# A two-layer linear-attention and gated-MLP kernel on one core: operations ordered by longest chain, and normalized rows transposed by DMA behind the first normalizations

## Chip, core and metric

The kernel runs on one core of a Trainium2 chip. The metric is device time of the whole program in microseconds (us). The time before is 454.07 us, the median of three runs (452.1, 454.07, 454.61). The engines are called as the profile calls them: PE (TensorE matmul), PEld (its weight load), DVE (VectorE), ACT (ScalarE), POOL (GpSimd), SP (SyncE, which here only issues DMAs).

## The reference

`x` is 2048 rows of 512 bf16 numbers. Two blocks alternate, A, B, A, B, with the same weights in both layers. `A_w_phi` holds one 16x16 matrix for each of 32 heads.

```python
def _A_ref(x, wqkv, w_phi, wo):                       # H = 32 heads of 16
    q, k, v = ((x @ wqkv) ... split into heads)
    pq = einsum("bhsd,hdf->bhsf", q, w_phi);  pk = einsum("bhsd,hdf->bhsf", k, w_phi)
    phi_q = concatenate([softmax(pq), softmax(-pq)]);  phi_k = concatenate([softmax(pk), softmax(-pk)])
    kv  = einsum("bhsf,bhsd->bhfd", phi_k, v);         z = sum of phi_k over s
    num = einsum("bhqf,bhfd->bhqd", phi_q, kv)
    den = einsum("bhqf,bhf->bhq", phi_q, z) + 1e-6
    return (num / den) ... heads joined ... @ wo

def _B_ref(x, W_gate, W_up, W_down):                  # F = 1376
    return (relu(x @ W_gate) * (x @ W_up)) @ W_down

x = x + _A_ref(layernorm(x), ...);  x = x + _B_ref(layernorm(x), ...)
x = x + _A_ref(layernorm(x), ...);  x = x + _B_ref(layernorm(x), ...)
```

`kv` and `z` sum over all 2048 rows, so no row can pass the second half of A before every row has passed the first half.

## The kernel before

**Tiling.** The rows are 16 tiles of 128, and 4 stages (`st`) of 4 tiles. All weights and `x` (`x_sb`) stay in SBUF. One row of work for a stage is this:

- `layernorm(st)` (lines 400 to 441). On DVE, per tile: statistics (line 404, 405), then for the four tiles together twelve tiny operations that make 1/sqrt(variance) by bit trick and two Newton steps (lines 415 to 423), then one `ytile <- x_sb` per tile (line 429, "apply"). PE transposes each `ytile` in four 128x128 blocks into one PSUM bank (line 318), and DVE (odd tiles, line 437) or ACT (even tiles, line 440) copies the bank into `yT`, which has rows of x along the free axis. `ytile` has 4 buffers, `yT` has 6 (each for a whole stage).
- `keys(st)`: per tile 4 + 4 matmuls of 128x512 (`Wkp`, `wv`), two exponentials on ACT (line 464), their sum and its reciprocal on DVE (466, 468), a copy of v on ACT (472), v over the sums on POOL (475); then 32 small matmuls `vhat,expk` that give this stage's share of `kv` and `z`, added into `kvsum` on DVE (488, 491).
- `sums()`: DVE turns `kvsum` into two matrices, `ZDw` and `kvbd` (500, 503). It needs all four stages.
- `queries(st)`: 16 matmuls with `Wqp` and eight exponentials on ACT (513). `Wqp` and `Wkp` are products of the weights with `w_phi`, made once at the start (`fold`).
- `attend(st)`: 32 tiny matmuls `ZDw,expq`; a chain on DVE (`Zs`, `zm`, `zden`, reciprocal `zr`, `atok`, lines 530 to 537); 4 PE transposes of `atok` and a copy `aT` (542); 8 matmuls `aT,EC`, each followed by a DVE multiply into `expq` (547, "em"); 8 matmuls `expq,kvbd`, copied to `oT` by ACT (552); 16 matmuls `wo_sb,oT`, each four of them added into `x_sb` on DVE (561, "residual").
- `glu(st)`: 88 matmuls with `Wg` and `Wu`, 11 relus on ACT (576), 11 multiplies on DVE (578), 44 matmuls `Wd,hT`, four residuals on DVE (561). All 88 need the four tiles of `yT`.

**Order.** The kernel does not write the instruction streams by hand. `op` and `dma` record operations with what they read and write and with an estimated occupancy and latency in ns; a `Program` derives dependences, lays all operations out in time (`schedule`) and makes from that the in-order stream and the semaphore waits of each engine (`plan`, `emit`). `schedule` takes, at each step, the operation that can begin first by its own estimates; among equals, the one recorded first (`prio` is the index). It also gives out the eight PSUM banks at that time, so an operation can wait for a bank that another stage's operation still reads. What is laid out is fixed: on the chip each engine runs its stream in order and waits at each semaphore.

The order in which operations are recorded (lines 602 to 617): layer 1's `layernorm` and `keys` of stages 0 to 3; then in each layer `sums`, queries and attend of stage 0 with the normalization behind it, and in turn queries and attend of stage st+1 (with its normalization), `glu(st)`, and the next layer's `layernorm` and `keys` of stage st (or, in layer 2, the four output DMAs of stage st, on SP). So there are 16 normalizations of a stage: 4 ahead of layer 1's keys, 4 ahead of layer 1's glu, 4 ahead of layer 2's keys, 4 ahead of layer 2's glu. SP has nothing to do between the loads at the start and the 16 output DMAs.

Of the kernel before, what the change touches and what calls it, by code (L numbers as in the profile page):

```python
# [42 lines left out]
class Op:  # L43
    __slots__ = ("idx", "eng", "fn", "reads", "writes", "occ", "lat", "name", "is_dma", "nbytes",
                 "deps", "odeps", "users", "missing", "ready", "start", "finish", "cnt", "stream", "prio")

    def __init__(self, idx, eng, fn, reads, writes, occ, lat, name, is_dma=False, nbytes=0):
        self.idx, self.eng, self.fn = idx, eng, fn
        self.reads, self.writes = list(reads), list(writes)
        self.occ, self.lat, self.name = float(occ), float(lat), name  # L50
        self.is_dma, self.nbytes = is_dma, nbytes
        self.deps, self.odeps, self.users = set(), set(), []
        self.missing, self.ready = 0, 0.0
        self.start = self.finish = self.cnt = self.stream = None
        self.prio = idx


class Program:
    SYNC = 120.0
    SAME = 60.0  # L60
# [12 lines left out]

    def dma(self, eng, fn, reads=(), writes=(), nbytes=0, name=""):
        o = Op(len(self.ops), eng, fn, reads, writes, self.DMA_ISSUE[eng], 0, name, True, nbytes)
        self.ops.append(o)
        return o

# [37 lines left out]

    def schedule(self):
        self.derive()
        free = {e: 0.0 for e in ENGINES}
# [3 lines left out]
        left = len(self.ops)  # L123
        for o in self.ops:
            if not o.missing:
                ready[o.eng].append(o)
# [4 lines left out]
        while left:  # L131
            best = None
            for e in ENGINES:
                for o in ready[e]:
                    s = max(free[e], o.ready)
                    if best is not None and s > best[0] and s > free[e]:
                        continue
                    b = new_bank(o)
                    if b is not None:
                        if not banks:  # L140
                            continue
                        s = max(s, min(banks)[0])
                    key = (s, o.prio)
                    if best is None or key < best[:2]:
                        best = (s, o.prio, o)
            assert best is not None, "no operation can go on"
            s, _, o = best
            ready[o.eng].remove(o)
            b = new_bank(o)
            if b is not None:  # L150
                entry = min(banks)
                banks.remove(entry)
                b.bank = entry[1]
                old = entry[2]
                if old is not None:
                    for x in old.ops:
                        if x.eng != "pe":
                            o.deps.add(x.idx)
            o.start = s
            if o.is_dma:  # L160
                free[o.eng] = s + o.occ
                begin = max(s + 0.35 * self.DMA_LAT, qfree)
                qfree = begin + o.nbytes / self.DMA_BW
                o.finish = qfree + 0.65 * self.DMA_LAT
            else:
                free[o.eng] = s + o.occ
                o.finish = s + o.lat
            for r in set(o.reads) | set(o.writes):
                if isinstance(r, Bank):
                    r.left -= 1  # L170
                    if not r.left:
                        t = max(x.finish + (0.0 if x.eng == "pe" else self.SYNC) for x in r.ops)
                        banks.append((t, r.bank, r))
            for u in o.users:
                if o.idx in u.deps:
                    t = o.finish + (self.SAME if u.eng == o.eng and not o.is_dma else self.SYNC)
                    u.ready = max(u.ready, t)
                u.missing -= 1
                if not u.missing:
                    ready[u.eng].append(u)  # L180
            left -= 1
# [57 lines left out]
def build_kernel(nc, A_x, A_wqkv, A_w_phi, A_wo, W_gate, W_up, W_down, out):  # L239
# [8 lines left out]
    with ExitStack() as ctx:  # L248
# [58 lines left out]
        op, dma = prog.op, prog.dma  # L307
# [4 lines left out]
        def mm(ps, view, lhsT, rhs, start, stop, reads, n, name):  # L312
            lat = 0.4167 * n + 167
            op("pe", lambda e: e.matmul(view(ps), lhsT, rhs, start=start, stop=stop),  # L314
               reads=reads, writes=[ps], occ=max(25.0, 0.4167 * n + 2.6), lat=lat, name=name)

        def tr(ps, view, src, reads, name):
            op("pe", lambda e: e.transpose(view(ps), src, ident[:]),  # L318
               reads=list(reads) + [R("ident")], writes=[ps], occ=56, lat=220, name=name)
# [4 lines left out]
        def b16half(ps):  # L324
            return ps.b16()[:, 0:512]

# [8 lines left out]
        def load_x(t0, t1):  # L335
# [27 lines left out]
           reads=[R("mask8a")], writes=[R("mask8")], occ=150, name="mask8")  # L363
        op("pool", lambda e: e.affine_select(EC[:].rearrange("p g (h j) -> p g h j", j=16), ones[:].rearrange("p (g h j) -> p g h j", g=8, j=16),
                                             [[-8, 8], [-1, 8], [0, 16]], ALU.is_equal, 0.0, base=0, channel_multiplier=1),
# [35 lines left out]
        def layernorm(st):  # L401

            for t in range(4 * st, 4 * st + 4):
                op("dve", (lambda t: lambda e: e.bn_stats(stats[:, t, :], x_sb[:, t, :]))(t), reads=[R("x", t)], writes=[R("st", t)], occ=580, lat=680, name=f"bn{t}")  # L404
                op("dve", (lambda t: lambda e: e.bn_aggr(mv[:, t, :], stats[:, t, :]))(t), reads=[R("st", t)], writes=[R("mv", t)], occ=70, lat=172, name=f"ba{t}")  # L405
            ts = range(4 * st, 4 * st + 4)
            var = mv[:, 4 * st:4 * st + 4, 1:2]
            y = rstd[:, 4 * st:4 * st + 4, :]
            v, hx, t1 = rsv[:, st], rsh[:, st], rst[:, st]
            Rmv, Ry, Rv, Rh, Rt = [R("mv", t) for t in ts], [R("rs", t) for t in ts], [R("rv", st)], [R("rh", st)], [R("rt", st)]  # L410

            def small(fn, reads, writes):
                op("dve", fn, reads=reads, writes=writes, occ=65, lat=160, name="rstd")

            small(lambda e: e.tensor_scalar(v, var, float(EPS_LN), None, op0=ALU.add), Rmv, Rv)
            small(lambda e: e.tensor_scalar(hx, var, 0.5, 0.5 * float(EPS_LN), op0=ALU.mult, op1=ALU.add), Rmv, Rh)
            small(lambda e: e.tensor_single_scalar(t1.bitcast(I32), v.bitcast(I32), 1, ALU.logical_shift_right), Rv, Rt)
            small(lambda e: e.tensor_scalar(y.bitcast(I32), t1.bitcast(I32), -1, 0x5F3759DF, op0=ALU.mult, op1=ALU.add), Rt, Ry)
            for _ in range(2):
                small(lambda e: e.tensor_tensor(t1, y, y, ALU.mult), Ry, Rt)  # L420
                small(lambda e: e.tensor_tensor(t1, t1, hx, ALU.mult), Rt + Rh, Rt)
                small(lambda e: e.tensor_scalar(t1, t1, -1.0, 1.5, op0=ALU.mult, op1=ALU.add), Rt, Rt)
                small(lambda e: e.tensor_tensor(y, y, t1, ALU.mult), Ry + Rt, Ry)
            b = cnt["yT"] % NYT
            cnt["yT"] += 1
            for t in ts:
                yb = cnt["y"] % NY
                cnt["y"] += 1
                op("dve", (lambda t, yb: lambda e: e.tensor_scalar(ytile[:, yb, :], x_sb[:, t, :], mv[:, t, 0:1], rstd[:, t, :], op0=ALU.subtract, op1=ALU.mult))(t, yb),  # L429
                   reads=[R("x", t), R("mv", t), R("rs", t)], writes=[R("y", yb)], occ=320, lat=405, name=f"apply{t}")  # L430
                ps = bank(f"ytr{t}")
# [4 lines left out]
                if tt % 2:  # L436
                    op("dve", (lambda ps, dst: lambda e: e.tensor_copy(dst, b16half(ps).rearrange("p (c n) -> p c n", c=NC)))(ps, dst),
                       reads=[ps], writes=[R("yT", b, tt)], occ=328, lat=415, name=f"ycp{t}")
                else:
                    op("act", (lambda ps, dst: lambda e: e.activation(dst, b16half(ps).rearrange("p (c n) -> p c n", c=NC), ACT.Copy))(ps, dst),  # L440
                       reads=[ps], writes=[R("yT", b, tt)], occ=480, lat=600, name=f"ycp{t}")
# [5 lines left out]
        def keys(st, b):  # L447
# [30 lines left out]
            for g0, g1 in ((0, 3), (3, 6), (6, 8)):  # L478
# [8 lines left out]
                if st == 0:  # L487
                    op("dve", (lambda ps, dst, n: lambda e: e.tensor_copy(dst, ps.f32()[:, 0:n]))(ps, dst, n),  # L488
                       reads=[ps], writes=[R("kvs", g0)], occ=490, lat=580, name="kvs")
# [26 lines left out]
        def attend(st):  # L516
# [13 lines left out]
            op("dve", lambda e: e.tensor_copy(Zs[:, g], zdv(zd)[:, :, 0]), reads=[zd], writes=[R("Zs", g)], occ=330, lat=420, name="Zs")  # L530
# [11 lines left out]
            op("dve", lambda e: e.tensor_copy(aT[:, g, :], b16half(pa)), reads=[pa], writes=[R("aT", g)], occ=328, lat=415, name="aT")  # L542
            for c in range(NC):
# [8 lines left out]
                op("act", (lambda c, pn: lambda e: e.activation(oT[:, g, c, :], full(pn), ACT.Copy))(c, pn), reads=[pn], writes=[R("oT", g, c)], occ=480, lat=610, name=f"oT{st}")  # L552
# [49 lines left out]
        for st in range(NS):  # L602
            into_a(st)
# [71 lines left out]
```

## Time and profile before

| | |
|---|---|
| runs | 452.1, 454.07, 454.61 us; median 454.07 |
| profiled execution | 453.24 us; its span in the profile is 451.5 us, so 1.74 us lie around the span |
| PE (matmul records) | 419.7 us, 93% of the span |
| DVE | 331.3 us, 73% |
| ACT | 182.0 us, 40% |
| POOL | 72.9 us, 16% |
| chain that ended last, by engine | PE 77%, DVE 19%, DMA 1%, ACT 1% |
| DMA | 10.95 MB, nearly all in the first 20 us |

A "busy" PE is not PE at its peak, since matmuls are pipelined and the record of one overlaps the next: a 128x512 matmul has a record of 379 ns, and they follow each other faster than that. PE's idle time is therefore read from the weight-load records (PEld), whose starts give the pace. Idle time in front of an instruction is given with what ended it: "[4.51 <-DVE aT L542]" is 4.51 us of idleness that ended when DVE's copy of line 542 was done.

### The profile page before, as it was taken

What the parts mean: (1) busy time and instruction counts of PE and PEld (TensorE: products, weight loads), DVE (VectorE), ACT (ScalarE), POOL (GpSimd) and SP (SyncE); (2) the same over time, 40 slices, a digit from 0 to 9 for tenths busy, and PEclk for the clock granted to TensorE, in tenths of its full rate; (3) what the DMA queues carried; (4) which work ended last, traced back from release to release, by engine and by line L of the source; (5) the groups of instructions that cost most, each with busy time, mean ns of one, the idle gap of its engine ahead of it and who ended that gap; (6) DMA issues with size and microseconds to landing.
All of it is one profiled execution on the core that took longest, in us unless ns stands there. A gap on an engine that the chain in (4) does not pass through costs nothing.

```text
span 451.5 us, 6587 instructions
## 1 busy us (share of the span) xinstructions
PE 419.7 (93%) x2512; PEld 211.2 (47%) x2560; DVE 331.3 (73%) x819; ACT 182.0 (40%) x329; POOL 72.9 (16%) x75
## 2 busy tenths in 40 slices
PE   3969899789999999999999999887999999999997
PEld 2545556334544544444445444632454454444443
DVE  5999977999669956997578476799963863883342
ACT  4768687223406440453145249622340340341230
POOL 3335780000000700070007005100000000000000
PEclk9999999979999999999999999988999999999999
DMA  8930000000000000000000000000001001000001
GB/s 260 384 107 1 0 1 2 1 0 1 0 1 2 1 1 0 2 0 1 0 1 1 1 0 1 1 1 1 0 2 46 1 0 37 12 1 23 23 1 46
DMA packets 9567, 10.95 MB, mean 24 GB/s; under 512 B 992, under 2 KB 8512, under 8 KB 9536
## 3 DMA queue, kind: packets, MB, share of 16 engines
q1 hardware_dynamic: 7952, 9.47, 6.1%
q10 hardware_dynamic: 1584, 1.07, 0.8%
q8 instruction: 20, 0.33, 0.3%
q14 instruction: 11, 0.09, 0.1%
HBM read 8.44 MB, written 2.10 MB: 23 GB/s over the span
## 4 chain that ended last, share of the span: by engine, by line
PE 77%; DVE 19%; DMA 1%; issue 1%; ACT 1%; POOL 0%; SPq 0%
PE pb L314 74%; DVE expq L547 4%; PE pb L318 3%; DVE stats L404 3%; DVE x_sb L561 2%; DVE Zk L466 1%; DMA x_sb<-in_A_x_dram 1%; DVE kvsum L491 1%; DVE ytile L429 1%; DVE zr L535 1%; DVE hT L578 1%; DVE kvsum L488 1%; DVE kvbd L503 0%; DVE mv L405 0%; DVE Zs L530 0%
## 5 line engine op out<-in xcount | busy, mean ns | idle before, releaser
L576 ACT ACTIVATE gate_sb<-pb 128x512 bf16<-128x512 f32 (+1 forms) x88 | 52.5, 596 | 138.3 <-PE pb L314 136.0
L475 POOL TENSOR_TENSOR vhat<-vsb,rZk 128x544 bf16<-128x544 bf16 x64 | 68.5, 1102 | 210.6 <-DVE rZk L468 195.4
L578 DVE TENSOR_TENSOR hT<-gate_sb,pb 128x512 bf16<-128x512 bf16 (+1 forms) x88 | 59.8, 680 | 44.0 <-PE pb L314 43.8
L314 PE MATMUL pb<-yT,Wg 128*128 128x512 bf16 (+1 forms) x340 | 91.1, 379 | 0.4
L314 PE MATMUL pb<-yT,Wu 128*128 128x512 bf16 (+1 forms) x345 | 91.1, 379 | 0.3
L314 PE MATMUL pb<-Wd,hT 128*128 128x512 bf16 (+1 forms) x344 | 77.0, 379 | 0.4
L561 DVE TENSOR_TENSOR x_sb<-x_sb,pb 128x512 bf16<-128x512 bf16 x64 | 42.2, 683 | 47.0 <-PE pb L314 47.0
L314 PEld LDWEIGHTS pb<-Wd,hT 128*128 128x128 bf16 (+1 forms) x352 | 34.3, 98 | 41.5
L314 PEld LDWEIGHTS pb<-yT,Wu 128*128 128x128 bf16 (+1 forms) x352 | 34.8, 100 | 37.2
L314 PEld LDWEIGHTS pb<-yT,Wg 128*128 128x128 bf16 (+1 forms) x352 | 34.7, 100 | 36.5
L552 ACT ACTIVATE oT<-pb 128x512 bf16<-128x512 f32 x32 | 18.9, 597 | 68.6 <-PE pb L314 68.5
L404 DVE BATCH_NORM_STATS2 stats<-x_sb 128x6 f32<-128x512 bf16 x64 | 42.6, 675 | 1.0 <-DMA x_sb<-in_A_x_dram 0.5
L466 DVE TENSOR_REDUCE Zk<-expk 128x64 f32<-128x1024 bf16 x32 | 37.9, 1190 | 5.4 <-ACT expk L464 5.3
L547 DVE TENSOR_TENSOR expq<-expq,pb 128x512 bf16<-128x512 bf16 x64 | 41.2, 677 | 0.9 <-PE pb L314 0.9
L513 ACT ACTIVATE expq<-pb 128x512 bf16<-128x512 f32 x64 | 33.0, 623 | 18.9 <-PE pb L314 18.8
L464 ACT ACTIVATE expk<-pb 128x512 bf16<-128x512 f32 x64 | 35.0, 602 | 9.6 <-PE pb L314 6.9
L314 PE MATMUL pb<-wo_sb,oT 128*128 128x512 bf16 x125 | 34.4, 379 | 0.3
L314 PE MATMUL pb<-Wkp,yT 128*128 128x512 bf16 x121 | 32.7, 383 | 0.6 <-issue 0.2
L314 PE MATMUL pb<-wv,yT 128*128 128x512 bf16 x126 | 32.7, 379 | 0.1
L314 PE MATMUL pb<-yT,Wqp 128*128 128x512 bf16 x121 | 30.9, 379 | 0.2
L314 PE MATMUL pb<-aT,EC 128*128 128x512 bf16 x64 | 21.7, 460 | 9.6 <-DVE aT L542 9.5
L314 PE MATMUL pb<-vhat,expk 128*128 128x136 bf16 x256 | 25.0, 223 | 3.3 <-POOL vhat L475 2.9
(59 smaller groups left out, 378.0 us busy)
## 6 DMA issues: line engine op xcount, KB each, us to landing
out_dram<-x_sb SPq DMA_DIRECT2D x16, 128.0 KB, 1.7
x_sb<-in_A_x_dram SPq DMA_DIRECT2D x3, 512.0 KB, 10.0
Wg<-in_B_W_gate_dram SPq DMA_DIRECT2D x1, 1376.0 KB, 11.9
Wu<-in_B_W_up_dram SPq DMA_DIRECT2D x1, 1376.0 KB, 12.9
Wd<-in_B_W_down_dram SPq DMA_DIRECT2D x1, 1280.0 KB, 16.1
hT<-in_A_wqkv_dram ACTq DMA_DIRECT2D x1, 512.0 KB, 5.0
x_sb<-in_A_x_dram SPq DMA_DIRECT2D x2, 256.0 KB, 4.7
wv<-in_A_wqkv_dram ACTq DMA_DIRECT2D x1, 512.0 KB, 8.4
```

What stands on the lines that cost most here:

```text
L314: op("pe", lambda e: e.matmul(view(ps), lhsT, rhs, start=start, stop=stop), reads=reads, writes=[ps], occ=max(25.0, 0.4167 * n + 2.6), lat ...
L318: op("pe", lambda e: e.transpose(view(ps), src, ident[:]), reads=list(reads) + [R("ident")], writes=[ps], occ=56, lat=220, name=name)
L404: op("dve", (lambda t: lambda e: e.bn_stats(stats[:, t, :], x_sb[:, t, :]))(t), reads=[R("x", t)], writes=[R("st", t)], occ=580, lat=680, ...
L464: op("act", (lambda i, s, pk: lambda e: e.activation(expk[:, i, s, :], full(pk), ACT.Exp, scale=1.0 - 2.0 * s))(i, s, pk), reads=[pk], wri ...
L466: op("dve", (lambda i, zb: lambda e: e.tensor_reduce(Zk[:, zb, :], expk[:, i, :, :].rearrange("p s (h f) -> p (s h) f", f=16), AX.X, ALU.a ...
L475: op("pool", (lambda i, s, vb, rz: lambda e: e.tensor_tensor(vhat[:, i, s, :, :], vsb[:, vb, :, :], rZk[:, rz, s * 32:(s + 1) * 32].unsque ...
L513: op("act", (lambda c, s, ps: lambda e: e.activation(expq[:, st, c, s, :], full(ps), ACT.Exp, scale=1.0 - 2.0 * s))(c, s, ps), reads=[ps], ...
L547: op("dve", (lambda c, sg, ps: lambda e: e.tensor_tensor(expq[:, st, c, sg, :], expq[:, st, c, sg, :], full(ps), ALU.mult))(c, sg, ps), re ...
L552: op("act", (lambda c, pn: lambda e: e.activation(oT[:, g, c, :], full(pn), ACT.Copy))(c, pn), reads=[pn], writes=[R("oT", g, c)], occ=480 ...
L561: op("dve", lambda e: e.tensor_tensor(x_sb[:, t, :], x_sb[:, t, :], full(ps), ALU.add), reads=[R("x", t), ps], writes=[R("x", t)], occ=590 ...
L576: op("act", (lambda m, gb, pg: lambda e: e.activation(gate_sb[0:m, gb, :], pg.f32()[0:m, :], ACT.Relu))(m, gb, pg), reads=[pg], writes=[R( ...
L578: op("dve", (lambda m, gb, hb, pu: lambda e: e.tensor_tensor(hT[0:m, hb, :], gate_sb[0:m, gb, :], pu.f32()[0:m, :], ALU.mult))(m, gb, hb, pu),
```

## The change

1. `rank()` runs ahead of the layout: each operation gets the length of the longest chain of estimated latencies from it to the program's end, and `prio` is minus that. Among operations that can begin at the same time, the one with the longest chain goes first, not the one recorded first.
2. The planner's own estimates change: the time between an operation and its dependent now depends on the two engines (it was 120, or 60 on one engine), and PE's latencies are longer.
3. Some PSUM copies (`yT` copies of the first four normalizations, `kvsum` of stage 0, `Zs`, `aT`, `oT`) may be done by DVE or ACT; the planner takes the one that ends first.
4. `layernorm` has a flag. For the first four normalizations (`first=True`) PE transposes as before. For the other twelve, each `ytile` goes to `yT` by one transposing DMA from SBUF to SBUF, issued on SP: 48 DMAs of 128 KB. Their 192 PE transposes and 48 copies are gone.

The arithmetic is the same, but for half the variance, which is now taken from variance + eps and not from the variance by a second route.

```diff
+    def rank(self):
+        way = [0.0] * len(self.ops)
+        for o in reversed(self.ops):
+            lat = self.DMA_LAT + o.nbytes / self.DMA_BW if o.is_dma else o.lat
+            for u in o.users:
+                step = lat + self.sync(o.eng, u.eng) if o.idx in u.deps else o.occ
+                way[o.idx] = max(way[o.idx], way[u.idx] + step)
+            o.prio = -way[o.idx]
...
     def schedule(self):
         self.derive()
+        self.rank()
...
-                    key = (s, o.prio)
+                    key = (s, o.prio, o.idx)
...
+            if o.alts:
+                s, e = min((max(free[x], t) + o.alts[x][2], x) for x in o.alts for y, t in ready[x] if y is o)
+                o.eng = e
...
+        def copy(ps, dst, view, writes, dve, act, name):
+            either({"dve": (lambda e: e.tensor_copy(dst, view(ps)), dve, dve + 88), "act": (lambda e: e.activation(dst, view(ps), ACT.Copy), act, act + 120)},
+                   reads=[ps], writes=writes, name=name)
...
-        def layernorm(st):
+        def layernorm(st, first=False):
...
+                tt = t % 4
+                if not first:
+                    dma("sp", (lambda dst, yb: lambda e: e.dma_start_transpose(dst, ytile[:, yb, :]))(yT[:, b, :, tt * 128:(tt + 1) * 128], yb),
+                        reads=[R("y", yb)], writes=[R("yT", b, tt)], nbytes=131072, name=f"yT{t}")
+                    continue
                 ps = bank(f"ytr{t}")
                 for c in range(NC):
                     tr(ps, ..., ytile[:, yb, c * 128:(c + 1) * 128], [R("y", yb)], f"ytr{t}")
...
-                if tt % 2:
-                    op("dve", ... name=f"ycp{t}")
-                else:
-                    op("act", ... name=f"ycp{t}")
+                copy(ps, dst, lambda p: b16half(p).rearrange("p (c n) -> p c n", c=NC), [R("yT", b, tt)], 328, 480, f"ycp{t}")
...
         for st in range(NS):
-            into_a(st)
+            buf[st] = layernorm(st, first=True)
+            keys(st, buf[st])
```

The estimates of a DMA in the planner (2000 ns and 180 bytes per ns, 560 ns of SP to issue) are those of before, and the transposing DMAs get the same.

## Prediction

> **What bounds the kernel.** I read the utilization rows first, then the busy times of single stretches, then PE's weight loads in order of time.
>
> ```profile
> PE   3969899789999999999999999887999999999997
> DVE  5999977999669956997578476799963863883342
> PEclk9999999979999999999999999988999999999999
> ```
>
> PE is full but for three places: the start (slices 1 to 6), slices 8 and 9, slices 26 to 28. DVE is at 9 in nearly all of these, so there DVE sets the pace. Elsewhere PE does.
>
> ```profile
> 120.00:140.00 20.00, 19.89 (x96) 9.37 (x97) 13.40 (x35) 4.07 (x7) 0.00 (x0) 1.00 0.00 1
> 87.00:102.00 15.00, 10.35 (x50) 4.34 (x49) 14.28 (x41) 2.75 (x5) 0.00 (x0) 0.77 0.00 0
> 303.00:317.00 14.00, 9.74 (x48) 4.02 (x47) 13.83 (x42) 2.87 (x5) 0.00 (x0) 0.88 0.00 1
> ```
>
> After the span's stretch come PE, PEld, DVE, ACT, POOL busy (instructions), then the granted clock. In the middle of a layer PE issues all the time. Behind each layer's first attend, DVE is full, PE issues half as many, and the clock sinks to 0.77 and 0.88.
>
> ```profile
> 86.58 0.65 PEld L318 LDWEIGHTS pb<-ident,atok 128*128 128x128 bf16 x8
> 91.74 0.13 PEld L314 LDWEIGHTS pb<-aT,EC 128*128 128x128 bf16 x2 [4.51 <-DVE aT L542]
> 92.15 0.15 PEld L314 LDWEIGHTS pb<-aT,EC 128*128 128x128 bf16 x1 [0.28 <-issue]
> 92.58 0.15 PEld L314 LDWEIGHTS pb<-aT,EC 128*128 128x128 bf16 x1 [0.28 <-issue]
> 440.01 8.10 PEld L314 LDWEIGHTS pb<-Wd,hT 128*128 128x128 bf16 x38
> ```
>
> The last line gives PE's pace: 37 steps in 8.0 us, 0.2165 us for a 512-column matmul. After 4.51 us of idleness the steps are 0.43 us: half speed. The same view gives 0.071 us for a 136-column matmul, 0.028 for `ZDw,expq` and 0.056 for a 128x128 transpose.
>
> So PE's own work is 1696 x 0.2165 + 256 x 0.071 + 256 x 0.028 + 352 x 0.056 = 412.2 us (352: 256 transposes of `ytile`, 32 of `atok`, 64 in the weight folding). The span is 451.5, so 39.3 us are lost. Counting PE's work up to a marker and taking that from the marker's time places them: 10.5 before the first `Wkp` load (13.23 us), 6.4 from there to the first `ZDw` (69.69), 8.8 from there to layer 1's first glu transposes (101.4), 0.1 to layer 2's first `ZDw` (284.9), 10.4 to layer 2's first glu transposes (316.3), 0.2 to the last matmul, 2.9 behind it.
>
> **What goes.**
>
> ```profile
> L318 PE MATMUL pb<-ident,ytile 128*128 128x128 bf16 x256 | 22.2, 225 | 4.2 <-DVE ytile L429 4.0
> L440 ACT ACTIVATE yT<-pb 128x512 bf16<-128x512 bf16 x32 | 18.7, 607 | 13.8 <-PE pb L318 13.4
> L437 DVE COPY yT<-pb 128x512 bf16<-128x512 bf16 x32 | 12.6, 413 | 1.5 <-PE pb L318 1.5
> ```
>
> Of the 256 transposes 192 go: 192 x 0.056 = 10.7 us of PE, and PE is the bound, so this counts in full. PE's work becomes 401.5. By the changed program's order, copies into `yT` remain as 10 on DVE and 6 on ACT, and 13 other PSUM copies (6 `kvsum`, 5 `Zs`, 2 `aT`) move to ACT, one `oT` to DVE. ACT, busy for 40%, hides what it gets and gains nothing by what it loses. DVE's relief counts only in its three full stretches.
>
> **What the new order does to those stretches.** I lay DVE's order beside PE's order, for both programs. PE goes at its pace; a DVE operation begins when the one before it has ended and 0.25 us after the PE work it reads. DVE's steps, from the timeline: 0.59 us statistics, 0.6 residual, 0.6 em, 1.12 `Zk`, 0.45 `rZk`, 0.33 apply, 0.09 a tiny one, 0.87 `zr`. Where PE needs something that DVE has not ended, the difference is a stall. Before, this gives 4.3 us in the first keys, 7.2 at layer 1's first attend, 0.9 in the middle, 9.2 at layer 2's first attend: 21.6, where the trace shows 25.7. The 4.1 that it misses (half speed after idleness, ACT, POOL) I keep for both.
>
> For the changed program:
> - Start. Four statistics of stage 1 and their aggregates now stand inside stage 0's chain of tiny operations, 2.8 us of DVE more ahead of the applies. The chain is latency-bound (8.98 to 11.18 us for 12 operations of 0.09, so 1.1 us are gaps), and about 0.6 of it is absorbed: +2.2, so 12.7 instead of 10.5. Stage 1's 512 KB of x land 7.8 us after an issue at 1.8, so at 9.6, in time.
> - First keys: 3.8.
> - Layer 1's first attend: 7.5. The first glu matmul needs a PSUM bank that em of stage 2 reads, and that em stands on DVE behind the residuals and statistics of stage 1.
> - Attend of stage 3, and layer 2's keys: 2.6 + 0.5.
> - Layer 2's first attend. From the first residual to the last apply DVE has 4 residuals, 4 statistics, 4 aggregates, 12 tiny ones, 8 em, 2 `zm`, `zden`, `zr`, 4 applies: 13.7 us. Behind `wo_sb,oT` PE has 40 large matmuls, 33 `ZDw` and 2 transposes: 9.7 us. The residuals begin 0.45 before that, so the last apply ends 3.6 us too late, and then the DMAs come.
>
> **The transposing DMA** is in no row of before. Let D be the time from the end of a stage's last apply to the landing of its fourth DMA. Applies are 0.33 apart, so D = 3 x pace + landing - 1.0.
>
> ```profile
> out_dram<-x_sb SPq DMA_DIRECT2D x16, 128.0 KB, 1.7
> q1 hardware_dynamic: 7952, 9.47, 6.1%
> q10 hardware_dynamic: 1584, 1.07, 0.8%
> ```
>
> Lower end: it behaves as an output DMA of the same 128 KB (1.7 us), issued every 0.5 us as SP's first loads are: D = 2.2. In the changed program a transpose moves blocks of 16 rows by 128 columns, so 512 pieces of 256 bytes. A packet took 36 ns of an engine in q10 (0.8% of 16 x 451.5 us, over 1584) and 55 ns in q1. By 36 ns a transpose takes 512 x 36 / 16 = 1.2 us of the 16 engines and lands in 1.7 - 0.3 + 1.2 = 2.5 (0.3 being the output's own 128 packets): D = 5.1. By 55 ns: 1.8, 3.0, D = 7.3. Far end: 32-byte pieces, 9 us each, D near 37. I take 5.1, as q10's packets are the smaller ones.
>
> [...]
>
> Who waits: each DMA waits for its apply only, SP being otherwise idle; output DMAs that stand ahead of transposes wait for residuals that DVE does ahead of those applies anyway. Six of the twelve normalizations are used 8.9 us or more after the last apply. The others have: layer 1 stage 0, 6.2 (the bank wait above covers it); layer 1 stage 3, 5.1; layer 2 keys of stage 3, 6.6; layer 2 glu of stages 2 and 3, 4.7 and 4.5; layer 2 glu of stage 0, nothing. PE waits in order, so everything behind it waits too. `ytile` is reused after 6.6 us at the closest, more than D.
>
> Cost: 3.6 + D, and what D exceeds those five covers by. For 5.1: 8.7 + 0.4 + 0.6 = 9.7.
>
> **Sum.** 401.5 + 12.7 + 3.8 + 7.5 + 3.1 + 9.7 + 4.1 + 2.9 = 445.3 us of span. Around the span lie 453.24 - 451.5 = 1.74: 447.0, 1.4% under the profiled execution and 1.6% under the median of 454.07, which that execution undercuts by 0.2%.
>
> **Rivals.**
> - The DMAs are quick (D = 2.2): 5.8 instead of 9.7, 443.1 us. For it: 128 KB in 1.7 us. Against: four times as many pieces.
> - Slower: the transposing DMAs follow each other at 1.8 us or more on their one queue. At D = 7.3 the cost is 10.9 + 2.6 + 2.8 + 2.2 + 1.1 + 0.7 = 20.3: span 455.9, 457.6 us. Every us of D above 6.6 costs 6 us. The gain is gone at D = 6.5, 1.4 above my value; that is what makes slower likely at all. The place is PE idle in front of layer 2's first `yT,Wg`, ended by a DMA.
> - No change: the order gives back what the DMAs save. PE now has fewer query matmuls to fill the first keys (the folding of `Wqp` comes later), and the wait of 8.7 us lets the clock sink, so that 4 us behind it run at half speed. Some 6 us more in these two: 453 us. For it: the half-speed steps above. Against: the 4.1 kept holds part of it.
> - The change does what it says only off the path: excluded, since PE has no idleness from 102 to 285 us to hide 10.7 us in.
>
> **Numbers.** Forecast 447 with 0.38, quick DMAs 0.15, no change 0.15, slower 0.32 (0.04 of it far above the range). Within 0.5% of the median (451.8 to 456.3) is about what a measurement can't tell from no change. Faster 0.53, same 0.15, slower 0.32. The range goes from 440 (quick DMAs, and a start no later than before) to 464 (D near 8.3).
>
> **What would show it.** Right: 48 transposes landing in about 2.5 us; first `Wkp` load near 15.4 us; 8 to 9 us of stall between layer 2's first `wo_sb,oT` and its first `yT,Wg`, ended by a DMA, and none above 1 us in front of its other `yT,Wg`; layer 1's first glu released by DVE's em. Wrong: landings of 4 us and more, or repeated PE waits for `yT` in each glu; or a first-keys stretch that loses more than 6 us beyond the start.

## The result and the profile after

The changed kernel takes 469.0 us (median of four runs, 468.36 to 469.32) against 454.34 us of the kernel before beside it: ratio 1.0332, 95% interval 1.031 to 1.0353. It is slower by 3.3%; the prediction said 447.0 us, faster. The profiled execution took 468.88 us, its span is 467.1.

The utilization rows of the changed kernel, with POOL's row:

```profile
PE   3876999977999998989999959987799999999896
DVE  5999987997719669923965986879635559448242
POOL 3156582000000000000105757100000000000000
PEclk9988999997999999999999979998799999999999
```

PE is under 9 in slices 1 to 4, 9 and 10, 24, and 27 to 29, and at 8 in 16, 18 and 38. Slices 9, 10 and 27 to 29 are the first attend of each layer, full of holes before too. Slices 2 to 4 and 24 lie in the keys, where POOL works; before, only slice 3 of these was under 9. Nearly all that POOL does is `vhat` (68.8 of its 73.3 us): 64 operations of 1104 ns, 32 in each layer's keys.

What the prediction called lost time (span less PE's own work at its pace), by stage, for the kernels of this study. "Keys 1" goes from the first `Wkp` load to layer 1's first `ZDw`, "attend 1" to layer 1's first glu matmul, "middle" to layer 2's first `ZDw`, "attend 2" to layer 2's first glu matmul, "rest" to the last matmul. The last column counts DVE's waits for POOL: short operations that begin inside a `vhat` operation and last over 0.1 us longer than the fastest fifth of their group, and their excess in us.

| kernel | us | PE's work | start | keys 1 | attend 1 | middle | attend 2 | rest | tail | waits for POOL |
|---|---|---|---|---|---|---|---|---|---|---|
| before | 454.3 | 412.2 | 10.5 | 6.3 | 8.5 | 0.4 | 10.2 | 0.1 | 3.3 | 12, 6.5 |
| predicted | 447.0 | 401.5 | 12.7 | 3.8 | 7.5 | 3.1 | 9.7 | 0 | 2.9 | - |
| after | 469.0 | 401.5 | 12.4 | 11.8 | 7.8 | 15.1 | 9.4 | 4.9 | 4.3 | 27, 18.2 |
| e1 order only | 462.8 | 412.2 | 12.4 | 13.1 | 4.2 | 7.7 | 4.2 | 4.2 | 3.3 | 29, 19.1 |
| e2 DMA only | 456.6 | 401.5 | 10.5 | 6.5 | 12.1 | 1.2 | 16.5 | 1.7 | 4.3 | 16, 9.3 |
| e4 no ranking | 457.3 | 401.5 | 10.5 | 8.7 | 10.9 | 1.6 | 15.7 | 2.4 | 4.3 | 16, 8.9 |
| e9 e1 unlocked | 456.0 | 412.2 | 12.4 | 8.2 | 4.1 | 3.0 | 4.2 | 4.3 | 3.3 | 15, 9.3 |
| e10 estimates only | 459.2 | 412.2 | 10.4 | 8.9 | 7.2 | 5.6 | 8.5 | 0.9 | 3.3 | 18, 11.2 |
| e11 e10 aware | 450.8 | 412.2 | 10.8 | 6.0 | 7.6 | 0.3 | 8.5 | 0.9 | 3.3 | 5, 3.1 |
| e13 copies, unlocked | 450.5 | 401.5 | 12.4 | 8.9 | 7.6 | 5.2 | 7.3 | 1.2 | 4.3 | 14, 8.9 |
| e14 copies, first glu PE | 453.0 | 403.3 | 12.4 | 13.0 | 3.9 | 11.4 | 4.4 | -0.5 | 3.8 | 27, 18.4 |
| e15 copies, aware, first glu PE | 445.0 | 403.3 | 10.2 | 6.3 | 6.6 | 0.3 | 12.0 | 0.8 | 3.8 | 9, 5.8 |
| e16 e1 aware | 456.2 | 412.2 | 12.4 | 5.7 | 7.0 | 0.5 | 11.4 | 2.8 | 3.3 | 14, 8.9 |
| e17 before aware | 450.7 | 412.2 | 10.3 | 4.1 | 7.9 | -1.0 | 10.7 | 0.1 | 3.3 | 7, 3.1 |
| e18 e11 with 90 ns | 446.3 | 412.2 | 10.3 | 3.0 | 8.0 | -1.2 | 8.4 | -0.3 | 3.3 | 4, 3.0 |

(A stage can show -1, as the pace is rounded. The prediction also kept 4.1 us that it gave to no stage. Beside the experiments, the kernel before took 453.2 to 454.0 us. e12 has no row, since its one profiled execution was a slow one, of 553.18 us.) From before to after PE's work falls by 10.7 us as predicted; the lost time grows by 26.3, of which 5.5 lie in the first keys, 14.7 in the middle, 4.8 behind layer 2's first glu matmul. The 15.1 of the middle are, counted in the same way: 2.8 at half speed behind layer 1's first glu load, 2.6 at the attend of stage 3 (172 to 190 us), 1.6 at a landing (204.73), 7.6 in layer 2's keys (from 260 us on); the rest is smaller.

How layer 2's keys look: first DVE, then POOL, in the changed kernel's timeline. Columns: start and length in us, engine, line, operation.

```profile
259.75 0.62 DVE L472 TENSOR_SCALAR rsv<-mv 128x4 f32<-128x4 f32 x1
260.29 1.21 DVE L522 TENSOR_REDUCE Zk<-expk 128x64 f32<-128x1024 bf16 x1
261.42 1.07 DVE L474 TENSOR_SCALAR rst<-rsv 128x4 int32<-128x4 int32 x1
...
264.15 0.54 DVE L524 RECIPROCAL rZk<-Zk 128x64 f32<-128x64 f32 x1
264.61 0.80 DVE L478 TENSOR_TENSOR rst<-rst,rsh 128x4 f32<-128x4 f32 x1
265.33 1.21 DVE L522 TENSOR_REDUCE Zk<-expk 128x64 f32<-128x1024 bf16 x1
266.46 1.07 DVE L479 TENSOR_SCALAR rst<-rst 128x4 f32<-128x4 f32 x1
...
269.58 0.85 DVE L478 TENSOR_TENSOR rst<-rst,rsh 128x4 f32<-128x4 f32 x1
270.47 1.03 DVE L479 TENSOR_SCALAR rst<-rst 128x4 f32<-128x4 f32 x1
271.54 1.02 DVE L480 TENSOR_TENSOR rstd<-rstd,rst 128x4 f32<-128x4 f32 x1
272.59 2.12 DVE L485 TENSOR_SCALAR ytile<-x_sb,mv,rstd 128x512 bf16<-128x512 bf16 x4
274.64 0.57 DVE L546 TENSOR_TENSOR kvsum<-kvsum,pb 128x408 f32<-128x408 f32 x1
```

```profile
259.24 4.28 POOL L531 TENSOR_TENSOR vhat<-vsb,rZk 128x544 bf16<-128x544 bf16 x4 [7.95 <-DVE mv L470]
264.29 4.28 POOL L531 TENSOR_TENSOR vhat<-vsb,rZk 128x544 bf16<-128x544 bf16 x4 [0.77 <-DVE rst L477]
269.32 4.28 POOL L531 TENSOR_TENSOR vhat<-vsb,rZk 128x544 bf16<-128x544 bf16 x4 [0.75 <-PE pb L358]
```

A tiny operation on 128x4 numbers has a record of 0.16 us ahead of the first `vhat` operation, here in the kernel before, an apply 0.41:

```profile
10.58 0.16 DVE L421 TENSOR_TENSOR rst<-rst,rsh 128x4 f32<-128x4 f32 x1
10.78 0.17 DVE L422 TENSOR_SCALAR rst<-rst 128x4 f32<-128x4 f32 x1
11.18 0.41 DVE L429 TENSOR_SCALAR ytile<-x_sb,mv,rstd 128x512 bf16<-128x512 bf16 x1
```

In the changed kernel's keys the tiny one has up to 1.07, and the profile shows no idle time, since the wait is inside the operation. In its trace, 20 tiny operations began inside a `vhat` operation, and 18 were held: each ended 0.02 or 0.03 us after a `vhat` operation ended. The two others began in its last 0.06 us. Of the 172 that began elsewhere none took over 0.172 us. Each of the six applies that began inside was held, and ended 0.15 after. Three of five `ZDw` make up the 27. Other forms that began inside a `vhat` operation were not held: 0 of 14 `Zk`, 0 of 10 `rZk`, 0 of 9 statistics and aggregates. A multiply that reads PSUM (`hT`) was not held either: 0 of 8 before, 0 of 1 after.

The `kvsum` additions, which read PSUM too, were not held (0 of 13 in the changed kernel). Tiny operations with two inputs from SBUF were held (line 478: 5 of 5), and so were those with one (line 479: 3 of 3). Why these forms are held and the others not, no run here shows.

PE waits in order, so this is what it shows. The changed kernel's weight loads:

```profile
109.62 0.13 PEld L358 LDWEIGHTS pb<-yT,Wg 128*128 128x128 bf16 x2 [3.13 <-DVE expq L602]
110.03 0.15 PEld L358 LDWEIGHTS pb<-yT,Wg 128*128 128x128 bf16 x1 [0.28 <-issue]
...
204.73 0.34 PEld L358 LDWEIGHTS pb<-yT,Wg 128*128 128x128 bf16 x3 [1.94 <-issue]
...
275.25 0.10 PEld L358 LDWEIGHTS pb<-vhat,expk 128*128 128x128 bf16 x1 [4.53 <-DVE kvsum L546]
...
329.35 0.14 PEld L358 LDWEIGHTS pb<-yT,Wg 128*128 128x128 bf16 x2 [4.72 <-issue]
...
434.59 0.76 PEld L358 LDWEIGHTS pb<-yT,Wg 128*128 128x128 bf16 x5 [1.94 <-DMA yT<-ytile]
```

At 275.25 PE has waited 4.53 us for the `kvsum` of 274.64, which stood on DVE behind the held chain above. At 329.35 (and 204.73) it waits for a landing, as the list of waits says (us in total, times, longest); the row under it has the median us from issue to landing, 2.5 as predicted:

```profile
PE pb L358 <- DMA yT<-ytile: 9.3, 5, 4.7
```

```profile
yT<-ytile SPq DMA_TRANSPOSE x48, 2.5
```

The queue with these DMAs has, after its name, packets, MB and the share of the 16 engines' span that the packets took:

```profile
q1 hardware_dynamic: 34064, 15.77, 12.9%
```

### The profile page after: what moved, and what is told of

It reads as the page before. It is cut to its first block, busy times and chain, and to the rows that moved or that the text cites. A ratio compares the mean times of both kernels' runs of the same rounds, so it can differ in the third digit from the quotient of the medians.

```text
span 467.1 us, 6260 instructions
## 1 busy us (share of the span) xinstructions
PE 420.5 (90%) x2368; PEld 201.3 (43%) x2368; DVE 326.3 (70%) x785; ACT 170.6 (37%) x315; POOL 73.3 (16%) x75
## 3 DMA queue, kind: packets, MB, share of 16 engines
q1 hardware_dynamic: 34064, 15.77, 12.9%
q10 hardware_dynamic: 1584, 1.07, 0.8%
## 4 chain that ended last, share of the span: by engine, by line
PE 62%; DVE 31%; DMA 3%; ACT 2%; POOL 1%; issue 1%; SPq 0%; POOLq 0%
PE pb L358 62%; DVE Zk L522 5%; DVE stats L469 5%; DVE expq L602 4%; DVE x_sb L616 4%; DMA yT<-ytile 3%; DVE ytile L485 2%; DVE rZk L524 2%; DVE rst L478 1%; DVE rst L479 1%; ACT expq L568 1%; DVE hT L633 1%; ACT expk L520 1%; DVE rst L474 1%; DVE rstd L480 1%
## 5 line engine op out<-in xcount | busy, mean ns | idle before, releaser
L358 PE MATMUL pb<-yT,Wg 128*128 128x512 bf16 (+1 forms) x352 | 108.5, 391 | 11.7 <-DMA yT<-ytile 8.9
L358 PE MATMUL pb<-yT,Wu 128*128 128x512 bf16 (+1 forms) x352 | 108.0, 385 | 0.0
L531 POOL TENSOR_TENSOR vhat<-vsb,rZk 128x544 bf16<-128x544 bf16 x64 | 68.8, 1104 | 219.6 <-PE pb L358 159.8
L358 PE MATMUL pb<-Wd,hT 128*128 128x512 bf16 (+1 forms) x352 | 92.2, 379 | 1.1 <-DVE hT L633 1.1
L358 PEld LDWEIGHTS pb<-yT,Wg 128*128 128x128 bf16 (+1 forms) x352 | 35.5, 102 | 55.1 <-issue 10.3
L358 PE MATMUL pb<-Wkp,yT 128*128 128x512 bf16 x128 | 41.4, 412 | 0.4 <-DMA yT<-ytile 0.4
L520 ACT ACTIVATE expk<-pb 128x512 bf16<-128x512 f32 x64 | 33.6, 602 | 21.8 <-PE pb L358 21.6
L469 DVE BATCH_NORM_STATS2 stats<-x_sb 128x6 f32<-128x512 bf16 x64 | 40.3, 679 | 0.0
L358 PE MATMUL pb<-wv,yT 128*128 128x512 bf16 x128 | 36.1, 379 | 0.4 <-DVE kvsum L546 0.4
L358 PE MATMUL pb<-yT,Wqp 128*128 128x512 bf16 x128 | 33.9, 382 | 0.0
L373 ACT ACTIVATE oT<-pb 128x512 bf16<-128x512 f32 x31 | 18.4, 612 | 41.7 <-PE pb L358 41.6
L358 PE MATMUL pb<-vhat,expk 128*128 128x136 bf16 x256 | 27.0, 223 | 5.5 <-DVE kvsum L546 4.2
L358 PEld LDWEIGHTS pb<-vhat,expk 128*128 128x128 bf16 x256 | 19.3, 98 | 17.7 <-DVE kvsum L546 5.5
```

Source lines behind the costliest of these rows:

```text
L373: either({"dve": (lambda e: e.tensor_copy(dst, view(ps)), dve, dve + 88), "act": (lambda e: e.activation(dst, view(ps), ACT.Copy), act, ac ...
L520: op("act", (lambda i, s, pk: lambda e: e.activation(expk[:, i, s, :], full(pk), ACT.Exp, scale=1.0 - 2.0 * s))(i, s, pk), reads=[pk], wri ...
L531: op("pool", (lambda i, s, vb, rz: lambda e: e.tensor_tensor(vhat[:, i, s, :, :], vsb[:, vb, :, :], rZk[:, rz, s * 32:(s + 1) * 32].unsque ...
```

## Experiments

Two theories stood first. L: DVE's short operations wait for POOL, and the new order brings them together. D: the transposing DMAs cost the time. e5 to e8, which kept the transposing DMAs, gave no result; e9 and e11 to e15 ask the same with PE's transposes or plain copies. A ratio is against the kernel before measured beside it. Runs other than e3, e9, e12 and e13 lay the whole program out anew.

**e1: order only,** every normalization transposed by PE.

```diff
-                if not first:
+                if False:
```

> The changed kernel, with every normalization transposed by PE again: the longest-chain order, the new estimates and the flexible copies alone. Theory L (lock): DVE's short operations on SBUF wait for the end of the vhat operation that POOL is in; the trace of the changed kernel shows 27 such waits of 18 us (12 of 6.5 us before), and the new order causes them, by standing normalizations beside vhat. Then this kernel is slow without any DMA: laid out by the trace's durations with such waits it has about 22 us of them, and ends near 463 us (461 to 467). Theory D (DMA): the 15 us come from the transposing DMAs; PE's waits that end with one are 9.3 us in the changed kernel. Then this kernel is near before, 448 to 455 us.

Measured: 462.79 us, ratio 1.0194 (1.0169 to 1.0219). Without one DMA transpose, 8.8 of the 14.7 us are there, in the first keys and the middle. So D falls as the whole cause, and the time is the one that L expected. L is not the whole either: in lost time e1 has 9.8 us more than before, the changed kernel 26.3.

**e2: DMA only.** The kernel before, with the flag and the DMA of the diff in its `layernorm`.

> The kernel before, with the twelve later normalizations transposed by DMA, its order rule, estimates and fixed copies kept. Theory L: about 12 us of waits for POOL, and the DMA's landing in front of each layer's first glu: 458 us (455 to 462). Theory D: most of the 15 us are here too: 464 to 470 us.

Measured: 456.64 us, ratio 1.0058 (1.0038 to 1.0078). Keys and middle are within 1 us of before; attend 1 and 2 lose 3.6 and 6.3 us more, rest and tail 2.6: that takes back the 10.7 us and a little more. So in lost time the DMAs alone add 13.5 us, the order with its estimates and copies (e1) 9.8, both together 26.3. Its weight loads in front of the first glu of each layer:

```profile
107.02 0.13 PEld L314 LDWEIGHTS pb<-yT,Wg 128*128 128x128 bf16 x2 [3.07 <-DVE expq L552]
107.42 0.15 PEld L314 LDWEIGHTS pb<-yT,Wg 128*128 128x128 bf16 x1 [0.28 <-issue]
...
321.87 0.12 PEld L314 LDWEIGHTS pb<-yT,Wg 128*128 128x128 bf16 x2 [3.07 <-DVE expq L552]
```

No DMA is named: the planner put stage 2's `aT,EC` matmuls into the gap that it gave the landing, and the glu then waits for the banks that em reads. After 3.07 us of idleness the steps are 0.43 us again.

**e4: no ranking.**

```diff
         self.derive()
-        self.rank()
```

> The changed kernel without the ranking: among operations that can begin at the same time, the one recorded first goes first again; DMA transposes, new estimates and flexible copies kept. Theory L: about 12 us of waits for POOL in place of 18, 456 us (453 to 460). Theory D: the DMAs are all there, so the time stays at 464 to 470 us.

Measured: 457.3 us, ratio 1.0077 (1.0048 to 1.0105). All 48 DMAs are there and 11.7 us of the loss are gone.

**e3: vhat in four.**

```diff
-  lambda e: e.tensor_tensor(vhat[:, i, s, :, :], vsb[:, vb, :, :], rZk[...32 heads...], ALU.mult)
+  lambda e: [e.tensor_tensor(vhat[:, i, s, h:h + 8, :], vsb[:, vb, h:h + 8, :], rZk[...8 heads...], ALU.mult) for h in range(0, 32, 8)][-1]
```

> The changed kernel with each vhat operation given as four instructions of 8 heads each, one behind the other; all else, the order of every engine and every wait among it, stays. POOL does the same work. Theory L: a short operation of DVE waits for at most a quarter of the 1.10 us, so the 18 us of waits fall to 8 to 11, and the time to 457 to 462 us, the gain lying in the first keys (15 to 72 us) and in layer 2's keys (246 to 294 us). Theory D: no gain, 468 to 472 us, as four instructions are no faster than one.

Measured: 470.69 us, ratio 1.0372 (1.0339 to 1.0405): a miss for L, and in the range of D. Its waits for POOL did fall to about 10 us, but POOL's group shows the price, in the kernel with quarters:

```profile
L531 POOL TENSOR_TENSOR vhat<-vsb,rZk 128x136 bf16<-128x136 bf16 x256 | 96.3, 415 | 194.6 <-PE pb L358 159.1 <-DVE rst L477 16.7 <-ACT vsb L528 9.1
```

By busy time four quarters take 1.50 us (96.3 over 64) where one operation took 1.08 (68.8 over 64); PE's loads now wait 18.9 us for `vhat` (3.3 in the changed kernel). One wait took the place of another, so this run tells nothing against or for L.

**e9: the tiny operations in a form that does not wait.** On e1, so that the order is the ranked one and POOL's work stays; one of the twelve edits:

```diff
-                small(lambda e: e.tensor_tensor(tm, tm, hx, ALU.mult), Rt + Rh, Rt)
+                small(lambda e: e.reciprocal(tm, tm), Rt + Rh, Rt)
```

> The order-only kernel (every transpose on PE, 462.8 us), same order on every engine and same waits, with the twelve tiny operations of each normalization given as reciprocals of the same tiles (this leaves out eps, the square root and the Newton steps: rows are divided by their variance). No reciprocal has waited for POOL in a trace so far (0 of 10 in the changed kernel that began inside a vhat operation; of the other tiny ones 18 of 20 did). POOL's work stays. Theory L (lock): the tiny operations' waits for POOL go; applies and ZDw keep theirs. By the trace's durations 11 us less: 450 to 455 us. Theory O (the ranked order loses by itself, by fewer matmuls to fill with and more waits among PE, ACT and DVE, and the waits for POOL lie in its shadow): 460 to 464 us.

Measured: 455.99 us, ratio 1.0045 (1.0018 to 1.0071), 6.8 us under e1, 1 us above what L expected (its profiled execution, the fastest, took 453.43). A chain of tiny operations that took from 261.48 to 270.6 us in e1, of which these are four:

```profile
266.05 0.80 DVE L478 TENSOR_TENSOR rst<-rst,rsh 128x4 f32<-128x4 f32 x1
266.89 1.03 DVE L479 TENSOR_SCALAR rst<-rst 128x4 f32<-128x4 f32 x1
267.95 1.02 DVE L480 TENSOR_TENSOR rstd<-rstd,rst 128x4 f32<-128x4 f32 x1
269.00 1.03 DVE L477 TENSOR_TENSOR rst<-rstd 128x4 f32<-128x4 f32 x1
```

takes from 255.56 to 260.4 in e9:

```profile
258.56 0.52 DVE L520 RECIPROCAL rZk<-Zk 128x64 f32<-128x64 f32 x1
259.00 0.12 DVE L478 RECIPROCAL rst<-rst 128x4 f32<-128x4 f32 x1
259.15 0.18 DVE L479 RECIPROCAL rst<-rst 128x4 f32<-128x4 f32 x1
259.36 0.18 DVE L480 RECIPROCAL rstd<-rst 128x4 f32<-128x4 f32 x1
...
260.43 2.12 DVE L485 TENSOR_SCALAR ytile<-x_sb,mv,rstd 128x512 bf16<-128x512 bf16 x2
```

```profile
254.76 8.75 POOL L527 TENSOR_TENSOR vhat<-vsb,rZk 128x544 bf16<-128x544 bf16 x8 [0.65 <-DVE rZk L520]
```

POOL works throughout, and the eight reciprocals keep to 0.2 us; only the two applies, 2.12 us for some 0.7, still wait. In the traces the gain lies in the first keys (13.1 to 8.2) and the middle (7.7 to 3.0), where L put it; these 9.6 us are more than the 6.8 of the medians. Theory O falls as the account of this loss; a smaller loss of the order by itself shows in e16.

**e10 and e11: without ranking, and a planner that knows the wait.** e10 is e1 without `self.rank()`; e11 adds this, where `vhat_at` holds begin and end of each `vhat` operation laid out so far.

```diff
+    def unlocked(self, o, s):
+        if o.eng == "dve" and (o.name in ("rstd", "zdw") or o.name.startswith("apply")):
+            for a, b in self.vhat_at[-3:]:
+                if a < s < b:
+                    s = b
+        return s
...
-                    s = max(free[e], t)
+                    s = self.unlocked(o, max(free[e], t))
```

> The order-only kernel without the ranking: new estimates and flexible copies alone. Laid out, it has 15 us of waits for POOL in place of 22. Theory L: 455 to 460 us, between before and order-only. Theory O with the ranking as its cause: 450 to 454 us, as before.

> The kernel of the run before this one, and the planner knows the lock: a short operation of DVE that would begin inside a vhat operation is laid out at its end, so other work is put there. All operations as they are. Theory L: the 15 us of waits fall to some 4, and 7 to 11 us are gained: 447 to 452 us. Theory O: no gain, within 2 us of the run before this one.

Measured: e10 459.19 us, ratio 1.013 (1.0089 to 1.0172); e11 450.8, ratio 0.9915 (0.9881 to 0.9949). Even without ranking the new estimates and flexible copies fall into the waits (18, 11.2 us); knowing them brings them to 5, 3.1 us, and the kernel under before.

**e12 and e13: quicker DMAs, without and with the unlocked chain.** In e12 each transposing DMA is a plain one of the same tile; e13 adds e9's edit.

```diff
-  e.dma_start_transpose(dst, ytile[:, yb, :])
+  e.dma_start(dst, ytile[:, yb, :].rearrange("p (c n) -> p c n", c=NC))
```

> The changed kernel, same order and same waits, with each of the 48 transposing DMAs given as a plain DMA of the same 128 KB from ytile to yT, in rows of 256 bytes (this leaves out the transposition): it shows what a quicker landing is worth. Rival of the prediction (quick DMAs, D = 2.2 us): 443 us. Theory L: the waits for POOL stay, so this ends 5 to 11 us under the changed kernel at best: 457 to 464 us. If the DMAs were nothing to the time: 467 to 470 us.

> The kernel with plain copies (462.3 us; it leaves out the transposition) with the tiny operations of each normalization given as reciprocals (leaves out eps, the square root and the Newton steps). Order and waits as in the changed kernel. Theory L: the tiny operations' waits for POOL go, so 9 to 12 us less by the layout, 451 to 455 us. If the landing of the DMAs is all that remains of the loss once they are there: within 2 us of 462.

Measured: e12 462.26 us, ratio 1.0185 (1.0138 to 1.0231). e13 450.53, ratio 0.9934 (0.9904 to 0.9965), 11.7 us less. In e13 the copies are issued 0.69 us apart (transposes: 1.31) and land in 2.3 us, so D, as the prediction defined it, is 3 x 0.69 + 2.3 - 1.0 = 3.4 instead of 3 x 1.31 + 2.5 - 1.0 = 5.4. From the changed kernel to e12, two us of D are worth 6.7 us; from e12 to e13, the tiny operations' waits for POOL are worth 11.7.

**e14 and e15: no landing in front of the first glu.** On e12, stage 0's normalization ahead of each glu goes back to PE; e15 is that without ranking and with the planner of e11.

```diff
         def out_of_a(st):
...
-            return layernorm(st)
+            return layernorm(st, first=st == 0)
```

> The ranked kernel with plain copies (leaves out the transposition of ten normalizations) and with stage 0's normalization ahead of each glu transposed by PE: 32 transposes come back (1.8 us of PE). Theory: the wait for a landing in front of the first glu matmul, with half speed behind it, is the DMAs' cost, and it sums with the waits for POOL: by the layout 12 us less than 462, 449 to 455 us. Rival: the first glu waits for the applies and its bank anyway: 460 to 464 us.

> No ranking, a planner that knows the waits for POOL, and stage 0's normalization ahead of each glu by PE; plain copies for the other ten (leaves out their transposition). Both losses go, and 160 transposes (9.0 us of PE) are saved: 441 to 446 us, some 7 us below the kernel without DMAs and with the same planner (450.8). If the saved PE work is always lost elsewhere: 449 to 453 us.

Measured: e14 453.03 us, ratio 0.9986 (0.9969 to 1.0002), 9.2 us under e12 with 1.8 us of PE work put back. e15 445.04, ratio 0.9802 (0.9758 to 0.9847). So there are two losses that can be taken away singly, 11.7 us by e13 and 9.2 by e14. e14 still has 27 waits for POOL, 18.4 us, and 13.0 and 11.4 us in first keys and middle, while its attends have 3.9 and 4.4 us for the 7.8 and 9.4 of the changed kernel. Both together are worth 17.2 us in e15; that is less than their sum, though e15 drops the ranking too, and whether the two overlap is not shown. With both gone, the saved PE work shows: e15 lies 5.8 us under e11, which has the same planner and no DMAs.

**e16 to e18: what the ranking costs by itself, and the best full version.** e16 is e1 with `unlocked`; e17 is the kernel before with `unlocked`; e18 is e11 with one estimate changed:

```diff
-  op("dve", fn, reads=reads, writes=writes, occ=70, lat=160, name="rstd")
+  op("dve", fn, reads=reads, writes=writes, occ=90, lat=180, name="rstd")
```

> The order-only kernel (ranked, every transpose on PE, 462.8 us) with a planner that knows the waits for POOL. If the ranked order loses only by these waits: 449 to 453 us, like the kernel without ranking and with that knowledge (450.8). If the ranked order also loses by itself, since it stands all of layer 2's keys in one stretch that DVE and POOL cannot keep up with: 457 to 462 us; the layout by the trace's durations says this, 458 us with no wait for POOL counted.

> The kernel before, its estimates and fixed copies kept, and the planner lays a short operation of DVE that would begin inside a vhat operation out at that operation's end. Its trace has 12 waits for POOL of 6.5 us. Theory L: 2 to 4 us less, 449 to 452 us. If those waits hide behind PE: 453 to 455 us.

> The kernel of e11 (no ranking, every transpose on PE, planner that knows the waits for POOL, 450.8 us) with one number of the plan changed: a tiny operation of DVE occupies 90 ns, as the traces have it, not 70. By the layout 3 to 4 us less: 446 to 449 us, faster than before and after. If the plan's 20 ns do not matter: 449 to 452 us.

Measured: e16 456.23 us, ratio 1.0053 (1.003 to 1.0077); e17 450.67, 0.9937 (0.9909 to 0.9966); e18 446.34, 0.9848 (0.982 to 0.9877). e16 falls between the two forecasts. With the knowledge the ranked order loses 5.4 us against e11, not where I expected it (the middle is 0.5) but at the start (+1.6), attend 2 (+2.9) and the rest (+1.9). It keeps 14 waits for POOL, with 5.7 and 0.5 us of lost time left in first keys and middle. Against e1 it gains 14.6 us in these two and loses 10.0 at the attends, so more than the waits moved. e17 shows that before paid for them too. e18 computes everything, has no DMA transpose, and beats both kernels. Its rows:

```profile
PE   3979998799999999999999999978999999999997
POOL 4246870000001500070006007000000000000000
PEclk9999999989999999999999999998999999999999
```

POOL works in layer 2 as four short bursts, between glus, where before's order had them too, and the PE row has nines through all of them.

## Why the prediction was wrong

- PE's own work, 401.5 us: right. 2368 loads stand where 2560 stood.
- The transposing DMA: right in size, in part by luck. Landing 2.5 us as taken, pace 1.3 instead of 1.2, D = 5.4 instead of 5.1. But the 36 ns a packet behind 2.5 and 1.2 did not come true. By the row of q1 above, the 26112 packets more (a DMA has 512 of 256 bytes in the trace, as predicted, and 32 of 4 bytes) took 20 ns each (12.9% of 16 x 467.1 us less 6.1% of 16 x 451.5). By the prediction's formula that is 0.64 us a DMA and a landing in 2.0. The pace is near the record of one issue on SP instead, 1.27 us (median of 48). Beside e13's plain copies the landing is nearly the same (2.5 us, 2.3), the pace is not (1.31, 0.69).
- Start, 12.7 (measured 12.4; first `Wkp` load at 15.06, forecast 15.4), layer 1's first attend, 7.5 (7.8, ended by em as forecast), layer 2's first attend, 9.7 (9.4): right in size. In the last the agreement is partly luck: only 4.7 us, where 8 to 9 were forecast, are one stall that ends with a DMA; the rest are shorter waits for ACT, DVE and half speed.
- **First keys, 3.8: the step that failed**, with 11.8; and with it the 0.5 for layer 2's keys, with 7.6. (The 2.6 beside it, for the attend of stage 3, came true.) These two terms are 15 of the 21.8 us by which the span passed the sum. I laid DVE's order beside PE's with one duration for each operation, 0.09 us for a tiny one and 0.33 for an apply, and had POOL nowhere in it. The durations did not hold inside a `vhat` operation: 27 operations took 18.2 us more. e9 takes the tiny ones' waits away, in the same order, and gains 4.9 us in the first keys and 4.7 in the middle of its trace; e13 gains 11.7 us in all. The trace of before had 12 such waits, 6.5 us, and its row of line 417 has a mean of 280 ns where the like line 418 has 184; I read neither.
- "None above 1 us" in front of the other glus: wrong. The timeline has 1.94 us at 204.73, 1.80 at 397.75 and 1.94 at 434.59; the list of waits names a DMA for five waits of PE, 9.3 us together. The last two of the three lie in the 4.9 us of "rest". D itself came out as sized (the last apply in front of 434.59 ended at 429.10, so 5.5 us), which leaves the covers: I had counted 5.1, 4.7 and 4.5 us of PE work behind the last apply, and from its end to the wait there were 3.6, 3.8 and 3.6 us. Why was not traced.
- The tail, taken as unchanged, grew by 1.0 us (3.3 to 4.3). The rival "no change" named the first keys as the place but for another reason (fewer query matmuls to fill); e9 shows that the held chain is the larger part. What is left there in e9, 8.2, may hold the fill, but e16, ranked too, has 5.7. The rival of slower DMAs (457.6 us) did not happen.
- Not settled: the shares were measured with plain copies in place of the transposing DMAs. The changed kernel with the planner of e11, or with its first glu normalization on PE, was not tried. What the ranking's own 5.4 us consist of was not taken apart. e9 and e12 to e15 leave out part of the arithmetic, so their values differ; e11 and e16 to e18, which compute everything, point the same way. The granted clock over the span was 0.985 in e1's trace and 0.996 in e9's; how much of the gain is the waits themselves, and how much the half speed behind them, was not separated.

## What to carry to other kernels

An operation's duration from a profile was measured beside the neighbours that it had there (here a tiny one took 0.16 us alone, and up to 1.07 when it began inside a `vhat` operation): before moving DVE work in an order, look what POOL does at the new place, and whether a group's mean lies above its fastest members, because these waits inside operations (27, 18.2 us) were shown as busy time. A planner that lays streams out by estimates can be told of such waits in a few lines. That was worth 2.5 us on the kernel before (e17) and 8.4 from e10 to e11; with the change's estimates and copies and one estimate put right (e18), the kernel lies 6.9 us under before (453.2 to 446.3), without the new order and without fewer PE transposes. Ask of a DMA that replaces PE work whether its issue pace and landing (here 1.31 and 2.5 us) lie behind other work: the one place in each layer where they did not took back in e2 nearly all (9.9 us) of the 10.7 that all twelve had saved.

## What the runs showed of the hardware

- In the changed kernel's trace DVE's tiny and apply operations, 0.16 and 0.4 us by their records, were held to the end of the `vhat` operation of POOL that they began in (18 of 20 and 6 of 6; +0.02 and +0.15 us), tiny ones up to 1.07 us; reciprocals (0 of 10), reductions (0 of 14), statistics and aggregates (0 of 9) and operations with a PSUM operand (0 of 18) were not held.
- POOL's `vhat` operation shrank less than its elements did: its records have 1104 ns for 544 elements a partition (changed kernel), 415 for 136 (e3), so an estimate of 1.7 ns an element and 185 ns beside them (by the busy times above, 1.08 and 0.38 us, some 140 ns).
- A transposing DMA of 128 KB is issued every 1.31 us on SP's queue and lands in 2.5 (changed kernel); a plain SBUF-to-SBUF one in rows of 256 bytes every 0.69, and lands in 2.3 (e13).
